# Starting a dense projection pass beside the first stage of a convolution: loads, slots and instruction order

## The chip, the cores and the metric

The kernel runs on one core of a Trainium2 chip. The metric is device time in microseconds, taken as the median of several runs. Before the change it is 2254.98 us (three runs, 2247.01 to 2256.77). The profiled execution of the same kernel spans 2245.5 us; all stage times below are from that execution.

## What is computed

Two unrelated halves, side by side in the output. Half A is a long convolution: `kv = shift(k) * v` (a filter of four taps along the sequence), then `y = irfft(rfft(kv) * rfft(ssm_k)) + kv * ssm_D`, then `q * y`, for 2048 rows and 1024 columns. Half B is a recurrence over 64 segments of 32 rows with a memory of 8 rows:

```
for s in range(n_seg):
    h = concatenate([mem, xs], axis=1)          # 8 memory rows, 32 rows of x
    q, k, v = h @ Wq, h @ Wk, h @ Wv            # 32 heads of 128
    p = softmax(mask(q @ k.T * scale))
    o = (p @ v) @ Wo
    mem = o[:, :M]; outs.append(o[:, M:])
```

All inputs and outputs are bfloat16.

## The kernel before, in words

Half A is `a_kernel`, a Fourier transform in three stages. Stage 1 (lines 229 to 259) walks 16 row tiles. For each, TensorE transposes a tile of ssm_k (line 233), VectorE forms the shifted product u (lines 252 to 258), TensorE applies the first transform to both (line 223), ScalarE copies the result out of PSUM (line 225), and the sync queue stores it to the DRAM scratch tensors SK and SU (line 226). Ahead of the loop stand tables of sines, built on VectorE, ScalarE and GpSimd (lines 102 to 216). Stage 2 (lines 306 to 345) gathers sets of Kg and Ug from that scratch; it can begin only when all of it has been stored. For each of 33 units it does two small transforms, four products on VectorE (lines 326 to 329, the first is called pa), and two matmuls back (z, lines 341 and 343), and stores to SZ. Stage 3 (lines 371 to 380) reads SZ, makes y, multiplies by q and stores half A's output.

Half B is `b_kernel`. Ahead of its recurrence stands a dense pass over the last 8 rows of each segment, which are 512 rows in all and do not depend on the memory. XBT holds them transposed (lines 502 to 510). The weights are cut into chunks of 128 x 2048 (512 KB): chunk (m, kc, g) is matrix m (0 for K, 1 for Q, 2 for V), rows kc, half g of the heads. A group (m, g) needs 8 chunks. For each of 16 heads it does a chain of 8 matmuls of 128 x 512 into PSUM (line 554, tile kb_ps), a copy to a stage tile, alternately on ScalarE and VectorE (lines 542 and 544), and at its end one store of 2 MB into the DRAM tensor REC (line 559). Each run of bytes in that store is 128 columns, 256 bytes, long.

After each of the four K and Q groups come four x blocks (lines 528 to 535): a load of 128 rows of x into X_sb (two buffers; even blocks on the sync queue, odd ones on GpSimd's), 8 transposes (xt_ps), a copy to xt (two buffers), and a store to REC. Then come the V groups (line 573, vb_ps), whose results go to the DRAM tensor VBD. The recurrence (from line 750) then reads REC, VBD and the weights.

Of the 64 weight chunks, 21 do not fit and are streamed in every segment through a ring of six slots from the DRAM tensor WS (line 629). The others stay resident: 12 in the pool Wmid, which is open from the end of stage 1, 19 in Wres, whose space is free only after stage 3, and 12 in Wlate, loaded after the V groups. In the dense pass, chunks that have no resident place yet are loaded into a ring of 8 slots called pw. A streamed chunk is copied from there into WS on GpSimd's queue (line 523).

The order of the program text is not the order on the engines. A scheduler with its own cost estimates places the instructions of each engine when the program is built, except in the recurrence, where the order is written out by hand. Every engine, and every DMA queue's issuing engine, then works in its own order, and waits on semaphores. In the built program before, group (0, 0), 128 matmuls, lies beside stages 2 and 3; the groups (0, 1), (1, 0), (1, 1), all x blocks but one, and the V groups come after stage 3's last matmul.

The functions that the change touches, with the line numbers of the profile:

Of the kernel before, what the change touches and what calls it, by code (L numbers as in the profile page):

```python
# [9 lines left out]
BF = mybir.dt.bfloat16  # L10
# [21 lines left out]
def a_kernel(ctx: ExitStack, tc, q, k, v, shift_k, ssm_k, ssm_D, outa, spare, stage1_done):  # L32
# [32 lines left out]
    with ExitStack() as c1:  # L65
        cw = c1.enter_context(tc.tile_pool(name="a_cw", bufs=1, side="right"))
        io = c1.enter_context(tc.tile_pool(name="a1_io", bufs=3, side="right"))
        k0pool = c1.enter_context(tc.tile_pool(name="a1_k0", bufs=6, side="right"))
        wk = c1.enter_context(tc.tile_pool(name="a1_wk", bufs=3, side="right"))
        ps_big = c1.enter_context(tc.tile_pool(name="a1_ps", bufs=3, space=PSUM))  # L70
# [6 lines left out]
        v_i = cw.tile([128, NP, 32], I32, name="v_i")  # L77
        nc.gpsimd.iota(v_i[:], pattern=[[2, NP], [128, 32]], base=0, channel_multiplier=0)
# [4 lines left out]
        shflat = cw.tile([1, 4096], BF, name="shflat")  # L83
# [3 lines left out]
        KS = []  # L87
        for db in range(8):
            KS.append(spare())
            (nc.sync if db % 2 == 0 else nc.scalar).dma_start(KS[db][:], ssm_k[db * 128:(db + 1) * 128, :])  # L90
# [97 lines left out]
        for M, n in ((Mre, nxr), (Mim, nxi)):  # L188
            nc.gpsimd.memset(M[:], 0.0)
            aM = cw.tile([128, NP, 32], I32, tag="aM", name="aM")  # L190
            nc.vector.tensor_scalar(out=aM[:], in0=v_i[:], scalar1=p_mod32[:, 0:1], scalar2=n[:, 0:1], op0=ALU.mult, op1=ALU.add)
            nc.vector.tensor_scalar(out=aM[:], in0=aM[:], scalar1=4095, scalar2=None, op0=ALU.bitwise_and)
            sM = cw.tile([128, NP, 32], BF, tag="sM", name="sM")
            act_sin(sM[:], aM[:], 12)
            nc.gpsimd.memset(sM[32:64, 0, :], 0.0)
            for (r0, c0) in [(0, 0), (64, 32)]:
                nc.gpsimd.tensor_copy(M[r0:r0 + 64, :, c0:c0 + 32], sM[r0:r0 + 64])
# [6 lines left out]
        aNi = cw.tile([128, NS, 32], I32, name="aNi")  # L204
        nc.vector.tensor_tensor(out=aNi[:], in0=w_f[:].unsqueeze(2).to_broadcast([128, NS, 32]),
                                in1=kcol_f[:, 0:32].unsqueeze(1).to_broadcast([128, NS, 32]), op=ALU.mult)
        for N, ph in ((Nre, (1024, 0)), (Nim, (2048, 1024))):
            nc.gpsimd.memset(N[:], 0.0)
            aN = cw.tile([128, NS, 64], I32, tag="aM", name="aN")
            for x in range(2):  # L210
                nc.vector.tensor_scalar(out=aN[:, :, 32 * x:32 * x + 32], in0=aNi[:], scalar1=ph[x], scalar2=None, op0=ALU.add)
            nc.vector.tensor_scalar(out=aN[:], in0=aN[:], scalar1=4095, scalar2=None, op0=ALU.bitwise_and)
            sN = cw.tile([128, NS, 64], BF, tag="sM", name="sN")
            act_sin(sN[:], aN[:], 12)
            for (r0, c0) in [(0, 0), (32, 64), (64, 0), (96, 64)]:
                nc.gpsimd.tensor_copy(N[r0:r0 + 32, :, c0:c0 + 64], sN[r0:r0 + 32])
# [12 lines left out]
        for t in range(16):  # L229
            pt = ps_t.tile([128, 1024], BF, tag="ktp", name="k_tp")  # L230
            for db in range(8):
                src = KS[db][:].rearrange("p (n r) -> p r n", r=16)[:, t, :]
                nc.tensor.transpose(pt[:, db * 128:(db + 1) * 128], src, ident[:])
            kt = wk.tile([128, 1024], BF, tag="kt", name="kt")
            nc.scalar.copy(kt[:], pt[:])
            if t == 0:
                nc.vector.tensor_tensor(out=kt[0:1, :], in0=kt[0:1, :], in1=Drow[0:1, :], op=ALU.add)
            stage1(kt, t, SK1)
            K0 = k0pool.tile([128, 1024], BF, tag="K0", name="K0")
            load_rows(K0, k, t, 0, nc.sync)  # L240
            ktiles[t] = K0
            Vt = io.tile([128, 1024], BF, tag="Vt", name="Vt")
            load_rows(Vt, v, t, 0, nc.gpsimd)
            acc = wk.tile([128, 1024], BF, tag="uacc", name="uacc")
            for li, lag in enumerate((3, 2, 1, 0)):
                if t - lag >= 0:
                    Kl = ktiles[t - lag]
                else:
                    Kl = io.tile([128, 1024], BF, tag="Kx", name="Kx")
                    load_rows(Kl, k, t, lag, nc.sync)  # L250
                if li == 0:
                    nc.vector.tensor_tensor(out=acc[:], in0=Kl[:], in1=SH[:, lag, :], op=ALU.mult)
                else:
                    pr = wk.tile([128, 1024], BF, tag="prod", name="prod")
                    nc.vector.tensor_tensor(out=pr[:], in0=Kl[:], in1=SH[:, lag, :], op=ALU.mult)
                    nc.vector.tensor_tensor(out=acc[:], in0=acc[:], in1=pr[:], op=ALU.add)
            u = wk.tile([128, 1024], BF, tag="u", name="u")
            nc.vector.tensor_tensor(out=u[:], in0=acc[:], in1=Vt[:], op=ALU.mult)
            stage1(u, t, SU1)
# [123 lines left out]
def b_kernel(ctx: ExitStack, tc, x, mem0, Wq, Wk, Wv, Wo, outb, n_seg, run_a):  # L383
# [26 lines left out]
    first_used = [ch for m, g in groups for ch in resident if ch[0] == m and ch[2] == g]  # L410
    parts = [first_used[:N2], first_used[N2:N2 + N3]]
# [40 lines left out]

    c0p = ExitStack()
    pools = {}

    def stage1_done():
# [4 lines left out]
        pools["ps0"] = c0p.enter_context(tc.tile_pool(name="b0_ps", bufs=2, space=PSUM))  # L461
# [31 lines left out]
    run_a(pw, stage1_done)  # L493

    wres3 = ctx.enter_context(tc.tile_pool(name="b_wres", bufs=1, reuse_waits="tile"))
    for i, ch in enumerate(parts[1]):
        res[ch] = wres3.tile([128, 2048], BF, name=f"Wres{i}")[:]

    ps0 = pools["ps0"]
    with c0, c0p:  # L500
        xq = [nc.sync, nc.gpsimd]
# [10 lines left out]
        def group(m, g):  # L512
            ws = []
            for kc in range(8):
                ch = (m, kc, g)
                if ch in res:
                    nc.sync.dma_start(res[ch], dram_chunk(ch))
                    ws.append(res[ch])
                else:
                    t = pw()  # L520
                    nc.sync.dma_start(t[:], dram_chunk(ch))
                    if ch in streamed:
                        nc.gpsimd.dma_start(stream_src(ch), t[:])
                    ws.append(t[:])
            return ws

        def x_block(b):
            X_sb = st.tile([128, 1024], BF, tag="X_sb", name="X_sb")
            xq[b % 2].dma_start(X_sb[:], x[b * 128:(b + 1) * 128, :])
            tp = ps0.tile([128, 1024], BF, tag="ps0", name="xt_ps")  # L530
            for kc in range(8):
                nc.tensor.transpose(tp[:, kc * 128:(kc + 1) * 128], X_sb[:, kc * 128:(kc + 1) * 128], ident[:])
            xt = st.tile([128, 4, 8, SEG], BF, tag="xt", name="xt")
            nc.vector.tensor_copy(xt[:], tp[:].rearrange("p (k j t) -> p j k t", k=8, j=4))
            nc.gpsimd.dma_start(REC[:, 4 * b:4 * b + 4, 0:256], xt[:].rearrange("p s k t -> p s (k t)"))

        flip = [0]

        def evac(dst, src):
            flip[0] ^= 1  # L540
            if flip[0]:
                nc.scalar.copy(dst, src)
            else:
                nc.vector.tensor_copy(dst, src)

        nxb = 0
        for m in (0, 1):
            for g in range(2):
                ws = group(m, g)
                stage = st.tile([128, n_seg, 16, 8], BF, tag="stage", name="stage")  # L550
                for hl in range(16):
                    ps = ps0.tile([128, 512], F32, tag="ps0", name="kb_ps")
                    for kc in range(8):
                        nc.tensor.matmul(ps[:], lhsT=ws[kc][:, hl * 128:(hl + 1) * 128],
                                         rhs=XBT[:, kc].rearrange("p s t -> p (s t)"),
                                         start=(kc == 0), stop=(kc == 7))
                    evac(stage[:, :, hl, :], ps[:].rearrange("p (s t) -> p s t", t=8))
                o = 256 * (m + 1) + 128 * g
                nc.sync.dma_start(REC[:, :, o:o + 128], stage[:].rearrange("p s h t -> p s (h t)"))
                for _ in range(n_blk // 4):  # L560
                    x_block(nxb)
                    nxb += 1
# [17 lines left out]


# [352 lines left out]
def kernel(  # L934
# [22 lines left out]
    def run_a(spare, stage1_done):  # L957
        with ExitStack() as ctx_a:
            a_kernel(ctx_a, tc, A_q[0], A_k[0], A_v[0], A_shift_k, A_ssm_k, A_ssm_D, outa, spare, stage1_done)
# [41 lines left out]
```

## Time and profile before

| stretch | us | what runs in it |
|---|---|---|
| stage 1 | 0 to 124.4 | 16 row tiles; last transform matmul at 122.7 |
| gap | 124.4 to 138.5 | first gathers; XBT |
| stage 2 | 138.5 to 253 | 33 units, 50 kb matmuls between them |
| stage 3 | 253 to 305 | 64 y matmuls, the other 78 kb matmuls of the group |
| three groups and their x blocks | 305 to 439.1 | 384 kb matmuls, the remaining x blocks |
| V groups | 439.1 to 498 | 256 vb matmuls |
| late weights, ring start | 498 to 519 | 12 chunks and the first 6 of the ring |
| recurrence | 519 to 2245 | 64 segments, 1218 streamed chunks |

TensorE's share of busy time over the span is 77%, VectorE's 40%, ScalarE's 28%. These are means over stretches that differ in what bounds them, so the stretches are read one by one. A line of the profile that begins with SPq, ACTq or POOLq is an instruction that only issues a DMA; its duration is the time that the issuing engine was held, not that of the transfer.

### The profile page before, as it was taken

Reading aid. Unit: us, or ns where it says so; the run is one execution under the profiler, and the core shown is the slowest. Engines: PE = TensorE matmul, PEld = TensorE weight load, DVE = VectorE, ACT = ScalarE, POOL = GpSimd, SP = SyncE. Lnnn points to the kernel's source line nnn. Section 1 sums busy time; section 2 is a strip of 40 time slices with the busy share of each in tenths; the row PEclk is TensorE's granted clock in tenths of the full one; section 3 lists DMA queues with packets and bytes.
Section 4 is the critical chain, followed back from the end, with each engine's and each line's share of the span. In section 5 each row is a group of like instructions: output and inputs, shape, how many; then the busy total and the mean of one; then the engine's idle time right before and its main releaser. Section 6 shows DMA issues by size and latency. Waiting matters only on the chain. (4 is left out here: it accounts for less than half of the span.)

```text
span 2245.5 us, 81488 instructions
## 1 busy us (share of the span) xinstructions
PE 1738.0 (77%) x35636; PEld 932.4 (42%) x35636; DVE 889.0 (40%) x2702; ACT 630.7 (28%) x1111; POOL 429.2 (19%) x1115
## 2 busy tenths in 40 slices
PE   4667767886787877888888888887877878888886
PEld 2222223333444444444444444444444444444443
DVE  9948632122333333333333333333333333333333
ACT  5856301112222222222222222222222222222222
POOL 7123311100111111211111112111111111122111
PEclk9789989897999999999999999999999999999999
DMA  7999698649999999999999999999999999999997
GB/s 247 358 364 323 216 323 276 171 112 395 392 393 370 388 391 380 388 389 387 396 391 395 395 392 390 393 393 381 394 385 369 383 391 392 386 389 390 392 390 266
DMA packets 293133, 803.59 MB, mean 358 GB/s; under 512 B 84812, under 2 KB 84844, under 8 KB 292775
## 3 DMA queue, kind: packets, MB, share of 16 engines
q1 hardware_dynamic: 262440, 734.16, 86.2%
q0 software_dynamic: 23536, 50.51, 6.6%
q10 hardware_dynamic: 6800, 13.72, 1.8%
q8 instruction: 278, 4.55, 0.8%
q14 instruction: 79, 0.65, 0.1%
HBM read 738.87 MB, written 62.39 MB: 357 GB/s over the span
## 5 line engine op out<-in xcount | busy, mean ns | idle before, releaser
L777 PEld LDWEIGHTS <-rec 128*32 128x32 bf16 x12351 | 319.5, 96 | 475.1 <-issue 255.1
L777 PE MATMUL acc<-wring,rec 128*32 128x512 bf16 (+1 forms) x3777 | 374.3, 386 | 136.9 <-DMA wring<-WS 121.8
L786 ACT CAST qkv_sb<-acc 128x512 bf16<-128x512 f32 x384 | 225.1, 586 | 672.0 <-PE acc L777 672.0
L777 PE MATMUL acc<-Wres,rec 128*32 128x512 bf16 x4864 | 382.3, 383 | 0.0
L863 PEld LDWEIGHTS <-OT 128*32 128x32 bf16 x8192 | 215.3, 96 | 174.8 <-issue 148.7
L777 PE MATMUL acc<-Wmid,rec 128*32 128x512 bf16 x3072 | 237.8, 384 | 0.9 <-issue 0.9
L863 PE MATMUL yacc<-Wlate,OT 128*32 128x256 bf16 x5120 | 219.6, 273 | 12.4 <-issue 11.4
L863 PE MATMUL yacc<-wring,OT 128*32 128x256 bf16 x3072 | 153.3, 275 | 97.0 <-DMA wring<-WS 57.4
L723 PEld LDWEIGHTS <-OTB 128*16 128x16 bf16 x4096 | 104.3, 89 | 104.7 <-issue 96.3
L879 DVE COPY KT<-tps 128x512 bf16<-128x512 bf16 x64 | 27.2, 425 | 291.2 <-PE tps L792 291.2
L849 ACT CAST OT<-OTp 128x512 bf16<-128x512 f32 x128 | 75.0, 586 | 236.9 <-PE OTp L841 236.7
L678 POOL DMA_DIRECT2D rec<-REC x64 | 37.3, 583 | 531.8 <-issue 270.3
L850 DVE CAST OTB<-OTp 128x128 bf16<-128x128 f32 x128 | 37.3, 291 | 255.3 <-ACT OT L849 255.3
L618 DVE TENSOR_SCALAR wring<-OTp 128x384 int32<-128x384 int32 x126 | 112.2, 891 | 59.7 <-PE acc L777 54.1
L753 POOL COPY KT<-rec 128x128 bf16<-128x128 bf16 x128 | 38.5, 301 | 454.5 <-PE SB L801 436.3
L723 PE MATMUL SB<-Wlate,OTB 128*16 128x256 bf16 x2480 | 95.7, 274 | 35.8 <-DVE SB L714 19.7
L807 DVE TENSOR_REDUCE mx<-SB 128x5 f32<-128x200 f32 x128 | 47.1, 368 | 190.4 <-PE SB L801 190.4
L738 POOL DMA_DIRECT2D out_dram<-YB x128 | 73.2, 578 | 233.6 <-DVE YB L736 220.1
L723 PE MATMUL SB<-wring,OTB 128*16 128x256 bf16 x1488 | 77.7, 273 | 39.4 <-DVE SB L702 32.9
L792 PE MATMUL tps<-ident,qkv_sb 128*128 128x128 bf16 x1024 | 101.2, 221 | 7.9 <-ACT qkv_sb L786 0.2
L792 PEld LDWEIGHTS <-qkv_sb 128*128 128x128 bf16 x1024 | 62.8, 97 | 105.5 <-ACT qkv_sb L786 63.4
L926 POOL DMA_DIRECT2D out_dram<-Y x64 | 45.5, 711 | 238.2 <-ACT Y L919 227.1
(216 smaller groups left out, 2412.6 us busy)
## 6 DMA issues: line engine op xcount, KB each, us to landing
wring<-WS SPq DMA_DIRECT2D x1218, 512.0 KB, 7.3
rec<-REC POOLq DMA_DIRECT2D x64, 192.0 KB, 6.1
SK<-s_sb SPq DMA_DIRECT2D x16, 512.0 KB, 5.3
SU<-s_sb SPq DMA_DIRECT2D x16, 512.0 KB, 4.8
Kg<-SK ACTq DMA_DIRECT2D x32, 256.0 KB, 5.5
Ug<-SU SPq DMA_DIRECT2D x32, 256.0 KB, 5.6
REC<-stage SPq DMA_DIRECT2D x4, 2048.0 KB, 18.1
SZ<-zs SPq DMA_DIRECT2D x31, 256.0 KB, 5.2
```

The lines of the kernel that those rows point to most:

```text
L618: nc.vector.tensor_scalar(out=dst, in0=src, scalar1=0, scalar2=None, op0=ALU.bitwise_or)
L678: nc.gpsimd.dma_start(rec[:], REC[:, s, :])
L723: nc.tensor.matmul(self.acc[32 * dq:32 * dq + W, x - o:y - o], lhsT=self.OTB[:, c, 4 * g + i, :], rhs=r, start=first and not self.seeded, ...
L738: nc.gpsimd.dma_start(bass.AP(outb.tensor, outb.offset + (SEG * NB * self.b + NX) * 2048 + 256 * dq, [[2048 * SEG, NB], [2048, 8], [1, 256 ...
L753: nc.gpsimd.tensor_copy(KT[:, :, :, 32:40], KBs[:, 128 * g:128 * g + 128].rearrange("p (c i t) -> p i c t", c=4, i=4))
L777: nc.tensor.matmul(self.acc[32 * c:32 * c + 32, x - 512 * c:y - 512 * c], lhsT=hT[:, kc, :], rhs=r, start=(kc == 0 and x == 512 * c), stop ...
L786: nc.scalar.copy(sb[:], self.acc[:])
L792: nc.tensor.transpose(tp[:, i * 128:(i + 1) * 128], sb[:, i * 128:(i + 1) * 128], ident[:])
L807: nc.vector.tensor_reduce(out=mx[:], in_=S, op=ALU.max, axis=AX.X)
L849: nc.scalar.copy(OT[:], o_view[:, :, :, 0:32])
L863: nc.tensor.matmul(yacc[32 * dq:32 * dq + 32, x - o:y - o], lhsT=OT[:, c, i, :], rhs=r, start=(h == 0 and x == o), stop=(h == 31), tile_po ...
L926: nc.gpsimd.dma_start(bass.AP(outb.tensor, outb.offset + SEG * s * 2048, [[256, 4], [2048, 32], [1, 256]]), Y[:])
```

## The change

The dense pass is to begin earlier. XBT and group (0, 0) are put where stage 1 ends, so that the scheduler can place them beside stage 1; the groups (0, 1), (1, 0) and (1, 1) follow beside and after stages 2 and 3. For this, weight slots and PSUM are needed while stage 1 runs. The V tiles of half A's first eight row tiles now use slots of the ring pw, and as each is used up, its slot takes a chunk of group (0, 0). The rows of ssm_k, which had lain in that ring, get a buffer of their own, paid for by fewer buffers in the other pools of stage 1. The sine tables' integers and the shift filter lie in the two stage tiles, which are free until the first group needs one.

Since Wmid now serves groups (0, 1) and (1, 0), and Wres the V chunks, eight K and Q chunks of Wres (`extra`) are loaded after their group has gone through, for the recurrence. The x blocks come in sets of five, five and six after three groups.

The core of the diff:

```diff
-        io = c1.enter_context(tc.tile_pool(name="a1_io", bufs=3, side="right"))
-        k0pool = c1.enter_context(tc.tile_pool(name="a1_k0", bufs=6, side="right"))
+        io = c1.enter_context(tc.tile_pool(name="a1_io", bufs=2, side="right"))
+        k0pool = c1.enter_context(tc.tile_pool(name="a1_k0", bufs=5, side="right"))
-        ps_big = c1.enter_context(tc.tile_pool(name="a1_ps", bufs=3, space=PSUM))
+        ps_big = c1.enter_context(tc.tile_pool(name="a1_ps", bufs=2, space=PSUM))
...
-        v_i = cw.tile([128, NP, 32], I32, name="v_i")
+        ints = slot16([128, 4096], I32, "ints")
+        v_i = ints[:, 0:32 * NP].rearrange("p (a b) -> p a b", b=32)
...
-        shflat = cw.tile([1, 4096], BF, name="shflat")
+        shflat = slot16([1, 4096], BF, "shflat")
-        KS = []
+        KS = cw.tile([128, 8, 2048], BF, name="KS_nat")
...
-            kt = wk.tile([128, 1024], BF, tag="kt", name="kt")
+            kt = wk.tile([128, 1024], BF, tag="kt", bufs=2, name="kt")
-            Vt = io.tile([128, 1024], BF, tag="Vt", name="Vt")
+            Vt = slot4()[:, 0:1024] if t < 8 else io.tile([128, 1024], BF, tag="Vt", name="Vt")[:]
...
-    first_used = [ch for m, g in groups for ch in resident if ch[0] == m and ch[2] == g]
-    parts = [first_used[:N2], first_used[N2:N2 + N3]]
+    own = {mg: [ch for ch in resident if ch[0] < 3 and (ch[0], ch[2]) == mg] for mg in groups}
+    parts = [(own[0, 1] + own[1, 0])[:N2], own[2, 0] + own[2, 1]]
+    extra = [ch for ch in own[0, 0] + own[1, 1] + resident if ch not in parts[0] + parts[1]][:N3 - len(parts[1])]
+    parts[1] = parts[1] + list(dict.fromkeys(extra))
...
     def stage1_done():
...
-        pools["ps0"] = c0p.enter_context(tc.tile_pool(name="b0_ps", bufs=2, space=PSUM))
+        make_xbt()
+        dense(0, 0)
...
-        nxb = 0
-        for m in (0, 1):
-            for g in range(2):
-                ws = group(m, g)
...
-                for _ in range(n_blk // 4):
-                    x_block(nxb)
-                    nxb += 1
+        for n, (m, g) in enumerate(((0, 1), (1, 0), (1, 1))):
+            dense(m, g)
+            for b in range(5 * n, min(5 * n + 5, n_blk)):
+                x_block(b)
+        x_block(n_blk - 1)
...
+        for ch in parts[1]:
+            if ch in extra:
+                nc.sync.dma_start(dst_view(res[ch], ch), dram_chunk(ch))
```

The tiles uacc, prod and u of stage 1 also go from three buffers to two. The recurrence is unchanged, but for which of its resident chunks lie in which pool.

## The prediction

> **What bounds the kernel now.** I read the table of stages first: one query for busy time, granted clock and DMA share in stretches cut at the stage borders (columns: stretch, its length, busy us and instructions of PE, PEld, DVE, ACT, POOL, then clock, DMA share, GB/s).
>
> ```profile
> 50.00:124.40 74.40, 44.34 (x166) 16.86 (x164) 60.60 (x112) 58.29 (x63) 10.18 (x19) 0.75 0.99 363
> 124.40:138.50 14.10, 6.03 (x40) 3.63 (x42) 0.00 (x0) 3.97 (x6) 1.08 (x2) 0.53 1.02 359
> 138.50:253.00 114.50, 88.80 (x445) 26.81 (x442) 96.31 (x173) 72.39 (x137) 45.72 (x43) 0.94 0.82 290
> ...
> 319.50:348.30 28.80, 28.80 (x130) 12.76 (x128) 5.53 (x8) 4.69 (x8) 3.68 (x6) 0.96 0.99 371
> 348.30:360.10 11.80, 3.10 (x35) 2.66 (x33) 2.67 (x4) 0.00 (x0) 2.58 (x4) 0.69 1.09 377
> 360.10:389.10 29.00, 29.00 (x129) 12.81 (x128) 5.53 (x8) 4.69 (x8) 3.13 (x5) 0.95 0.61 186
> 389.10:398.30 9.20, 3.12 (x33) 2.39 (x32) 1.98 (x3) 0.00 (x0) 2.05 (x3) 0.75 1.00 273
> 398.30:429.10 30.80, 29.98 (x129) 13.10 (x129) 6.22 (x9) 4.69 (x8) 2.61 (x4) 0.91 0.40 108
> 429.10:439.10 10.00, 3.08 (x34) 2.37 (x33) 2.67 (x4) 0.00 (x0) 2.04 (x3) 0.78 0.99 269
> ...
> 519.00:2245.00 1726.00, 1381.63 (x33981) 784.95 (x33981) 622.10 (x2240) 441.23 (x833) 301.25 (x953) 0.99 1.00 385
> ```
>
> The last row is the segment loop: DMA share 1.00, for 1726 us. It streams the same 1218 chunks before and after, so only its start can move. Ahead of it: stage 1 to 124.4 (from 50 us on its DMA share is 0.99), a gap of 14.1 in which stage 2 waits for its first gathers, stage 2 (114.5, DVE busy 96.3), stage 3 to 305, and then the tail, where PE alone works through dense groups of 29 to 31 us with sets of transposes of x (9 to 12 us, PE a third busy) between them, and the V pass until 498. In gap, groups, sets and V pass, one engine's delay is everybody's.
>
> Next, the instructions in order of time on the sync queue, to see what a set waits for (start, duration of the issue):
>
> ```profile
> 389.75 0.33 SPq L529 DMA_DIRECT2D X_sb<-in_B_x_dram  x1
> 390.18 0.52 SPq L559 DMA_DIRECT2D REC<-stage  x1
> 394.32 9.81 SPq L529 DMA_DIRECT2D X_sb<-in_B_x_dram  x1
> ...
> 300.23 0.57 SPq L559 DMA_DIRECT2D REC<-stage  x1
> 304.82 7.91 SPq L380 DMA_DIRECT2D out_dram<-ot  x2
> 313.15 0.87 SPq L529 DMA_DIRECT2D X_sb<-in_B_x_dram  x1
> ```
>
> An x load issued behind the 2 MB store of a group is stuck: at 394.32 its issue alone takes 9.81, until 14.0 after the store (404.13 - 390.18). Behind the store at 300.23 the x load goes out at 313.15 and PE, waiting for it, resumes at 317.73, 17.5 after the store. In the three later sets that late load is not needed: with two X_sb buffers a set of four needs two loads inside itself, and the one on SP is issued just ahead of the store.
>
> [...] a chain of 8 takes 1.73 us, a group of 128 takes 28.8. [...] The group's store writes runs of 256 B (128 columns of bf16), and the page's DMA part gives it 18.1 us for 2 MB (116 GB/s, against 385 in the loop).
>
> **The change, part by part.** I compared the order of instructions of the two built programs.
>
> 1. Stage 1. The ssm_k rows get their own buffer, V tiles 0 to 7 use the weight ring, the integer tables use the stage slots; several pools lose a buffer (K0 6 to 5, Kx 3 to 2, s1_ps 3 to 2). The 32 transposes for XBT and their 4 ACT copies (1.0 us each) move in, and 2 more weight chunks are loaded in it. The first table phase: shift filters now come after two kt copies, and the third Kx load waits for a Kx slot and for POOL's table copies (5.5 and 5.8 us), so u of row tile 1, at 40.4 before, moves to about 43. From there each tile takes 4.82 of DVE and 4.8 of ACT (1.03 + 4 x 0.94), and DMA is full. 2 chunks are 1 MB or 3 us at 363 GB/s; some V loads move out ahead of 50 us and give 1 to 2 back. 15 kb matmuls stand between the last s1 matmuls, and the eighth needs a chunk issued only after SU 13: up to 4 us of PE wait. I take +4; bounds 0 (all hidden in the waits that ACT has already) and +10.
>
> 2. The gap. After the last s1 matmul PE has 113 kb matmuls in a row ahead of the first Kre: 113 x 0.2157 = 24.4, plus about 1 for evacuations behind Kg issues on ACT. PE is in order, so stage 2's first products come some 27.5 after stage 1's last matmul (24.4 + 1 + the 2 that Kre, Ure and the copies take). Before: 138.56 - 122.7 = 15.9. So +11.5; bounds +9 and +14. This is what is paid for the group; the gap's 14 us are what is hidden.
>
> 3. Start of stage 2. The same 50 kb matmuls are spread over it as before. But group (0,1)'s two ring chunks need slots of (0,0), so are issued only at the end of the gap; PE meets them right behind unit 1, before the first z: about 3.5 of wait. Then SP issues the 2 MB store of (0,0) ahead of the first SZ stores and the fourth set's Ug: stuck for about 14, landing about 17 to 20 after, when three preloaded sets (6 units of 2.73 to 3.3) are used up: 0 to 5. Against that, the early stalls of DVE in this stage (idle 114.5 - 96.3 = 18 in all) shrink, as three sets are loaded. I take +2; bounds -7 and +8.
>
> 4. Stage 3: same order, same 78 kb beside it and just ahead. 0.
>
> 5. The tail. One group leaves it: the built order has 256 kb after the last y matmul, not 384: -29.5 (28.8, 29.0, 30.8: mean). The 16 x blocks are now in sets of 5, 5 and 6 behind three groups, not four sets of 4. So every set needs a third round of loads:
>  - set 1 (the rest of it 14.5 before): its fifth block is one more load, as at 318.79, issued behind two weight chunks: +3, and xt has two buffers, so that block's copy waits for the REC store of block 2: +1.5. Total 19.
>  - set 2: blocks 5 and 6 are ready, 7 comes by POOL, but 8 is on SP behind the store. Store at 1.1 after the group, landing of X_sb 17.5 later, two blocks more: about 21, not 11.8.
>  - set 3: two chunks (1 MB, 2.7 us) go ahead of the store, so block 12 lands at 1.1 + 2.7 + 17 = 20.5; block 14 can be issued only then and lands 4 later; 15 comes by POOL after the REC store of 12; the xt copies of 14 and 15 wait for stores of 12 and 13 (6 us to land): about 28, not 10.
>  Sets after: 19 + 21 + 28 = 68; before: 14.5 + 11.8 + 9.2 + 10.0 = 45.5: +22.5. Tail: -29.5 + 22.5 = -7. Bounds: -19 (17 and 20 for sets 2 and 3, 1.5 less in set 1) and +1.
>
> 6. The 8 extra chunks loaded a second time (4 MB, 11 us of DMA) lie in group and V pass, where DMA is 0.4 to 0.6 busy: 0, but for the chunk counted ahead of set 3's store. 12 late chunks and the ring's first 6 follow the V pass as before: 0. Other residents in the loop: same bytes streamed, 0.
>
> Sum: 4 + 11.5 + 2 + 0 - 7 = +10.5, which I round up to +12, since each wait leaves PE at the cold clock for its first chain (+1.7), and three such waits are new or longer. 2255 + 12 = 2267.
>
> **The rivals.** A: the group's removal is worth its full length and more, because the x loads land early: three sets of some 13 take 39 in place of 45.5, so the tail gains 36; with +11.5 in the gap and +4 in stage 1 it is -20.5: 2234. For it: the x loads are small and DMA is half idle there; set 3 and set 4 of before wait only 3 to 4 us at a time. Against: those loads stood ahead of the store in the ring. B: no change. The ring wait costs half (sets 2 and 3 together 38), because a store with nothing beside it drains in less than the 14 to 15.6 seen: tail -18, sum near +1: 2256. For it: the store of 430.16 was beside little traffic, and the rec load waited for it only until 445. Against: that is 15 us too. C: much slower: stage 1 is held by its smaller pools (+10) and stage 2 by the store at its start (+8), sum 10 + 14 + 8 - 7 = +25: 2280. For it: DMA at 0.99 in stage 1 and both new loads in it.
>
> **How the numbers follow.** My forecast 0.35, C 0.12, B 0.30, A 0.23. Slower by over 0.5% (above 2266.3) takes C and most of my own case, with its lower edge in "same": 0.44. Same (2243.7 to 2266.3): B and that edge, 0.33. Faster: A, 0.23. The likeliest is slower at 2267. The range goes down to 2238, leaving out the better half of A, and up to 2288, beyond C by its spread.
>
> **What would show it.** In the changed profile: 113 kb matmuls without a break in the gap and the first pa some 27 after the last s1 matmul (12 fewer if I am wrong on the gap); an X_sb issue of 9 us or more behind the stores of groups (1,0) and (1,1), with PE idle before xt_ps on DMA for some 12 in set 2 and 15 to 20 in set 3; V pass starting about 127 after the last y matmul, not 134. If sets 2 and 3 together take under 30, A is right. If pa comes later than 144 + 12 because stage 1's last matmul is past 132, it is C.

## The result, and the profile after

The changed kernel takes 2279.7 us (median of 4 runs, 2272.0 to 2288.4), the kernel before 2251.1 (median of 4, 2247.0 to 2256.8): ratio 1.0126, 95% interval 1.008 to 1.0173. It is slower, as forecast, but by 28.6 us between the medians, where 12 were forecast. The profiled executions have spans of 2245.5 and 2269.6, 24.1 apart; those 24 us can be placed.

First the table of stages of the changed kernel, cut at its own stage borders (columns as in the prediction).

```profile
50.00:138.00 88.00, 47.88 (x235) 22.23 (x234) 62.56 (x114) 63.41 (x70) 23.83 (x19) 0.92 0.89 320
138.00:165.00 27.00, 25.65 (x125) 11.49 (x124) 5.54 (x8) 6.32 (x11) 0.00 (x0) 1.00 0.98 357
165.00:284.50 119.50, 89.61 (x439) 27.00 (x436) 96.72 (x173) 71.43 (x136) 47.38 (x46) 0.92 0.84 285
...
388.00:409.00 21.00, 3.65 (x42) 3.10 (x41) 3.36 (x5) 0.00 (x0) 3.91 (x6) 0.65 0.94 250
409.00:437.80 28.80, 28.80 (x130) 12.80 (x129) 5.53 (x8) 4.68 (x8) 2.59 (x4) 0.96 0.19 57
437.80:464.30 26.50, 4.96 (x50) 4.14 (x49) 4.05 (x6) 0.00 (x0) 5.04 (x8) 0.58 0.97 276
543.80:2269.60 1725.80, 1385.62 (x33981) 790.91 (x33981) 622.73 (x2240) 440.69 (x833) 301.06 (x953) 0.99 1.00 385
```

The gap is now full of PE work, 25.65 of 27.0, and 27 long. The two later sets of x blocks (388 to 409 and 437.8 to 464.3) last 21 and 26.5 with PE busy for 4 to 5. Stage 1 ends at 138, and its DMA share fell to 0.89. The loop is what it was.

Read stage by stage, from the times of six instructions in each trace (end of the last stage 1 matmul, first product of stage 2, end of the last z matmul, end of the last y matmul, first V matmul, first recurrence matmul):

| us | stage 1 | gap | stage 2 | to last y | tail to V pass | V pass to loop | loop |
|---|---|---|---|---|---|---|---|
| before | 122.7 | 15.8 | 113.6 | 52.9 | 134.0 | 79.8 | 1726.6 |
| after | 138.0 | 27.1 | 119.4 | 53.3 | 126.5 | 79.5 | 1725.8 |
| difference | +15.3 | +11.3 | +5.8 | +0.4 | -7.5 | -0.3 | -0.8 |
| forecast | +4 | +11.5 | +2 | 0 | -7 | 0 | 0 |

Gap and tail came as forecast; stage 1 did not. The sync queue of the changed kernel, in order of time, as in the prediction:

```profile
164.71 0.52 SPq L562 DMA_DIRECT2D REC<-stage  x1
175.33 4.60 SPq L290 DMA_DIRECT2D SZ<-zs  x1
...
388.91 0.56 SPq L562 DMA_DIRECT2D REC<-stage  x1
389.56 13.23 SPq L533 DMA_DIRECT2D X_sb<-in_B_x_dram  x1
...
438.71 0.52 SPq L562 DMA_DIRECT2D REC<-stage  x1
439.33 13.56 SPq L533 DMA_DIRECT2D X_sb<-in_B_x_dram  x1
```

An x load behind a group's store holds SP for 13.2 and 13.6 us, and the first SZ store is done with its issue at 179.93, 15.2 after the store of group (0,0). PE's side of it, and of stage 1 (PE instructions in order of time; the bracket is the idle time before, and what ended it):

```profile
63.23 0.48 PE L512 MATMUL xbt_ps<-ident,X_sb 128*128 128x128 bf16 x3 [11.25 <-POOL ident masks.py:199]
...
80.69 0.50 PE L512 MATMUL xbt_ps<-ident,X_sb 128*128 128x128 bf16 x3 [7.33 <-DMA X_sb<-in_B_x_dram]
...
146.46 17.46 PE L557 MATMUL kb_ps<-XBT,pw 128*128 128x512 bf16 x80 [1.35 <-ACT stage L546]
163.85 0.41 PE L310 MATMUL Kre_ps<-Kg,Mre 128*64 128x512 bf16 x2
...
407.14 1.89 PE L536 MATMUL xt_ps<-ident,X_sb 128*128 128x128 bf16 x16 [13.84 <-DMA X_sb<-in_B_x_dram]
...
455.37 1.89 PE L536 MATMUL xt_ps<-ident,X_sb 128*128 128x128 bf16 x16 [16.06 <-DMA X_sb<-in_B_x_dram]
```

The first two lines are new and no step of the prediction has them: inside stage 1, PE stands for 11.3 us until POOL has built the identity, and for 7.3 until an x tile has landed, because the transposes for XBT are now in the middle of its queue. Behind it, DVE stalls in turn, first for PE and then for a K tile (its instructions in order of time):

```profile
62.34 0.68 DVE L259 TENSOR_TENSOR prod<-K,SH 128x1024 bf16<-128x1024 bf16 x1
67.89 0.69 DVE L262 TENSOR_TENSOR u<-uacc,pw 128x1024 bf16<-128x1024 bf16 x1 [4.86 <-PE s_ps L227]
...
78.52 0.69 DVE L259 TENSOR_TENSOR prod<-K,SH 128x1024 bf16<-128x1024 bf16 x1 [8.74 <-DMA K<-in_A_k_dram]
```

and POOL's instruction that PE waits for, first in the changed kernel, then in the kernel before:

```profile
47.49 15.69 POOL masks.py:199 TENSOR_SCALAR_AFFINE_SELECT ident<-ident 128x128 bf16<-128x128 bf16 x1
```

```profile
44.94 0.49 POOL masks.py:199 TENSOR_SCALAR_AFFINE_SELECT ident<-ident 128x128 bf16<-128x128 bf16 x1
```

It is the same instruction on the same 128 x 128 tile. It ends at 63.18, 0.16 after the DVE product of 62.34 ended. DVE stopped there because its next instruction waited for PE, and PE stood waiting for POOL.

### The profile page after: what moved, and what is told of

Same layout as the page of the kernel before. It is cut to its first block, busy times and chain, and to the rows that moved or that the text cites. A ratio compares the mean times of both kernels' runs of the same rounds, so it can differ in the third digit from the quotient of the medians.

```text
span 2269.6 us, 81502 instructions
## 1 busy us (share of the span) xinstructions
PE 1737.5 (77%) x35636; PEld 938.0 (41%) x35636; DVE 889.3 (39%) x2702; ACT 628.2 (28%) x1110; POOL 444.0 (20%) x1115
## 5 line engine op out<-in xcount | busy, mean ns | idle before, releaser
L794 PEld LDWEIGHTS <-rec 128*32 128x32 bf16 x12351 | 324.2, 96 | 467.0 <-issue 251.8
L794 PE MATMUL acc<-Wres,rec 128*32 128x512 bf16 x4864 | 395.7, 383 | 1.2 <-issue 1.1
L794 PE MATMUL acc<-Wmid,rec 128*32 128x512 bf16 x3072 | 224.9, 382 | 0.0
L740 PE MATMUL SB<-Wlate,OTB 128*16 128x256 bf16 x2480 | 97.2, 281 | 33.7 <-DVE SB L731 20.3
L943 POOL DMA_DIRECT2D out_dram<-Y x64 | 45.5, 711 | 239.6 <-ACT Y L936 236.6
```

What stands on the lines that cost most here:

```text
L740: nc.tensor.matmul(self.acc[32 * dq:32 * dq + W, x - o:y - o], lhsT=self.OTB[:, c, 4 * g + i, :], rhs=r, start=first and not self.seeded, ...
L794: nc.tensor.matmul(self.acc[32 * c:32 * c + 32, x - 512 * c:y - 512 * c], lhsT=hT[:, kc, :], rhs=r, start=(kc == 0 and x == 512 * c), stop ...
L943: nc.gpsimd.dma_start(bass.AP(outb.tensor, outb.offset + SEG * s * 2048, [[256, 4], [2048, 32], [1, 256]]), Y[:])
```

## The experiments

Each edit lets the scheduler place other instructions anew, so an edit in one stage can shift group matmuls in another; where that bears on a reading it is said. Single executions of one kernel differ by over 1% (55 of the kernel before lie between 2241 and 2273; in the profiled runs the loop alone takes 1721 to 1737), so totals are medians, and stages are read from the traces, one execution of each kernel. Counts of group matmuls in a stage are those recorded there; a few records are missing from each trace. A group matmul is counted as 0.2157 us: in the kernel before, those from 404.27 to 418.94 us start that far apart (14.67 us for 68, granted clock 1.00). Behind a set's wait for x they start further apart: 0.426 us in the kernel before from 399.50 to 402.91 (3.41 us for 8, granted clock 0.50 from 399.1 to 403.3), which is 1.7 more than a chain's 1.73 and is the prediction's cold clock. All of it in one table, the same columns as above; "ratio" is to the kernel before.

| run | stage 1 | gap | stage 2 | to last y | tail | median us | ratio (95%) |
|---|---|---|---|---|---|---|---|
| before | 122.7 | 15.8 | 113.6 | 52.9 | 134.0 | 2251 to 2256 | 1 |
| after | 138.0 | 27.1 | 119.4 | 53.3 | 126.5 | 2279.7 | 1.0126 (1.008-1.0173) |
| e1 | 134.4 | 26.0 | 119.8 | 55.4 | 124.3 | 2268.8 | 1.0072 (1.0053-1.0092) |
| e2 | 137.2 | 25.6 | 119.5 | 52.0 | 104.1 | 2253.6 | 0.9997 (0.9975-1.0018) |
| e3 | 139.2 | 13.5 | 105.5 | 53.9 | 145.0 | 2266.0 | 1.0057 (1.0038-1.0075) |
| e4 | 125.2 | 16.3 | 111.9 | 52.9 | 137.9 | 2257.5 | 1.001 (0.9986-1.0033) |
| e5 | 132.9 | 24.2 | 118.2 | 53.3 | 134.1 | 2274.1 | 1.01 (1.0081-1.012) |
| e6 | 138.2 | 25.6 | 123.8 | 55.7 | 92.6 | 2247.2 | 0.9971 (0.9956-0.9986) |
| e7 | 135.3 | 22.3 | 123.8 | 52.1 | 131.1 | 2265.8 | 1.0056 (1.0032-1.008) |
| b1 | 131.6 | 24.3 | 120.8 | 59.9 | 74.7 | 2225.0 | 0.9886 (0.9854-0.9918) |
| b2 | 122.4 | 16.5 | 110.5 | 53.6 | 108.7 | 2223.3 | 0.9871 (0.985-0.9891) |
| b3 | 136.8 | 22.3 | 121.3 | 55.4 | 73.7 | 2227.3 | 0.9874 (0.9827-0.9921) |
| b4 | 137.7 | 12.3 | 108.7 | 81.3 | 86.8 | 2235.0 | 0.9913 (0.9883-0.9943) |
| b5 | 126.2 | 24.2 | 123.2 | 57.0 | 82.8 | 2225.3 | 0.987 (0.9845-0.9895) |

**e1: the identity.** The changed kernel, with

```diff
-        make_identity(nc, ident[:])
+        nc.vector.tensor_copy(ident[:], a_ident[:])   # stage 1's own identity
```

> The changed kernel with one edit: the 128x128 identity that the XBT transposes read is copied on DVE from stage 1's own identity, not built on POOL. Theory 1 (in the changed kernel PE stands 11.3 us in stage 1 because POOL's 128x128 select for that identity is held off by DVE's back-to-back products, 15.69 us against 0.49 before, and the K loads issued late because of it cost DVE 8.7 more): the wait is gone, the last stage 1 matmul comes at 125 to 129 in place of 138.0, total 2270 (2264 to 2274). Rival (the smaller pools and the two added loads hold stage 1, and the identity's wait only covers that): last stage 1 matmul at 134 or later, total 2277 to 2282.

The wait for POOL is gone, yet stage 1 ends at 134.4, only 3.6 earlier and on the rival's side of the line. PE's queue in e1:

```profile
65.31 0.50 PE L512 MATMUL xbt_ps<-ident,X_sb 128*128 128x128 bf16 x3 [11.18 <-DMA X_sb<-in_B_x_dram]
```

The wait for an x tile, 7.3 before, has taken the identity's place. So the total fell into the expected range without the expected reason: the identity is one of two things that the same transposes lack, and taking one away lays the other bare.

**e2: the x loads.** The changed kernel, with

```diff
-        xq[b % 2].dma_start(X_sb[:], x[b * 128:(b + 1) * 128, :])
+        nc.gpsimd.dma_start(X_sb[:], x[b * 128:(b + 1) * 128, :])
```

> The changed kernel with one edit: all 16 x blocks are loaded by the POOL queue, so none stands in SP's ring behind a group's 2 MB store. Theory 1 (ring order is what makes sets 2 and 3 long): PE's wait of 13.8 us in set 2 and of 16.1 in set 3 falls to 3 to 6 each, set 2 from 21.0 to 11 to 15, set 3 from 26.5 to 14 to 18, total 2279.7 - 16 = 2264 (2258 to 2269). Rival (the 16 engines are busy with the store whatever queue the load comes from): waits of 11 or more stay, total 2276 to 2282. Stage 1 and the gap are as in the changed kernel.

PE's instructions are in the same order as in the changed kernel, so this is a clean comparison. Set 2 takes 14.0 (from 21.0), set 3 20.5 (from 26.5; 14 to 18 were expected), and the tail is 22 shorter. PE's waits for x loads in the tail fall from 50.8 us in all to 30.9, the longest from 16.1 to 6.4. Those in set 2 of e2:

```profile
378.52 1.03 PE L536 MATMUL xt_ps<-ident,X_sb 128*128 128x128 bf16 x8 [3.18 <-DMA X_sb<-in_B_x_dram]
381.68 1.03 PE L536 MATMUL xt_ps<-ident,X_sb 128*128 128x128 bf16 x8 [2.12 <-DMA X_sb<-in_B_x_dram]
386.81 1.03 PE L536 MATMUL xt_ps<-ident,X_sb 128*128 128x128 bf16 x8 [4.10 <-DMA X_sb<-in_B_x_dram]
```

A store of 2 MB in SP's ring (the DMAs that SP issues) holds up a load in POOL's much less than one behind it in its own: PE's three waits in this set are of 2.1 to 4.1 us, where one was 13.8 in the changed kernel. How the two rings are served side by side no run shows. The total fell by 26, to below the expected range, since set 1 gained too: its x load, issued at 344.09 in the changed kernel behind the store of group (0,1) and two out stores, made PE wait 10.4 there and 6.4 here.

**e3: the group put back.** XBT, buffers and weights as changed, but group (0,0) beside stages 2 and 3 and sets of four:

```diff
         make_xbt()
-        dense(0, 0)
...
     run_a(pw, slot16, stage1_done)
+    dense(0, 0)
```

> The changed kernel with the first group (K, half 0) put back beside stages 2 and 3, and x blocks in four sets of four; XBT, the buffers and the weight split stay as changed. Theory 1 (113 matmuls in the gap cost 11.2 us of it): first product of stage 2 comes 14 to 17 after the last stage 1 matmul in place of 27.1, stage 1 still ends near 138, last y matmul to V pass 134 in place of 126.7, total 2279.7 - 11.5 - 4 + 8 = 2272 (2267 to 2278). Rival (the gap is set by the gathers' round trip in the fuller DMA queues, the group lay in it for nothing): the gap stays at 24 or more and the total rises by the tail's 8, to 2286 or more.

The scheduler still put 46 of the group's 128 matmuls ahead of stage 2's first product, 30 of them in the gap. With 30 in place of some 113 the gap shrinks to 13.5, so it was the matmuls that made it 27.1, and the rival falls. Stage 2 shrinks as well, by 13.9, of which 34 fewer group matmuls in it (17, not 51) explain at most 34 x 0.2157 = 7.3. The tail grows by 18.5, to 145.0 where 134 was expected: the x loads, half of them still in SP's ring, make PE wait 43.6 there, 32.0 in the kernel before. Taken together what the early group adds costs 13.6 + 13.9 and saves 18.5. The total, 2266.0, is just below the expected range.

**e4: the small pools alone.** The kernel before, with

```diff
-name="a1_io", bufs=3 ... name="a1_k0", bufs=6 ... name="a1_ps", bufs=3
+name="a1_io", bufs=2 ... name="a1_k0", bufs=5 ... name="a1_ps", bufs=2
-tag="kt" / "uacc" / "prod" / "u"           (three buffers)
+tag="kt" / "uacc" / "prod" / "u", bufs=2
```

> The kernel before with nothing of the change but stage 1's smaller pools (Kx 3 to 2 with Vt, K0 6 to 5, kt, sums, products and u 3 to 2, PSUM 3 to 2). Theory 1 (pools cost little, a few us at the start): last stage 1 matmul at 123 to 127 (122.7 before), total within 4 us of the kernel before, 2251 to 2255. Rival (the pools are what made stage 1 15 us longer): last stage 1 matmul at 131 or later, total 2259 or more.

Stage 1 ends 2.5 later. The pools alone are a small part of the 15.3. The total is 2.5 above the expected range, and not told apart from the kernel before (0.9986 to 1.0033).

**e5: all x tiles of XBT loaded early.** e1, with

```diff
+        shflat = slot16([1, 4096], BF, "shflat")     # now ahead of the integers
...
+        XS = slot16([128, 4, 1024], BF, "XS")        # in the slot of the shift filters
         for tb in range(4):
-            X_sb = st.tile([128, 1024], BF, tag="X_sb", name="X_sb")
+            X_sb = XS[:, tb, :]
```

> Run e1 (identity copied on DVE) with one more edit: the four x tiles of XBT are loaded into one 8 KB tile in the slot that the shift filters leave at about 14 us, so no load waits for a transpose and all are sent while DMA is idle. Theory 2 (after e1: PE runs in order, and the XBT transposes inside stage 1 make it wait for whatever they lack, first the identity, without it X_sb, 11.2 us in e1): no wait for X_sb, last stage 1 matmul at 126 to 130 (134.4 in e1, 138.0 in the changed kernel), total 6 less than e1's 2269, 2263 (2258 to 2267). Rival (the K loads in a full DMA hold stage 1: DVE waits 12.3 us for them in e1): last stage 1 matmul at 133 or later, total 2266 to 2271.

Stage 1 ends at 132.9, the rival's side of the line: PE's wait for x fell to 6.5 in two pieces, and 10.2 of the 15.3 us were still there. The total, 2274.1, is above both ranges and 5 worse than e1's: the tail is 9.8 longer, with two more x blocks and 13 more group matmuls in it. Theory 2 falls as the whole explanation. What e5 and the kernel before have in common shows in one row of each, the stretch from 40 us to the end of stage 1 (first before, then after, then e5):

```profile
40.00:122.70 82.70, 50.57 (x196) 19.87 (x196) 70.60 (x125) 63.49 (x69) 17.49 (x30) 0.78 0.95 344
```

```profile
40.00:138.00 98.00, 53.47 (x252) 24.22 (x252) 72.56 (x129) 67.69 (x74) 33.73 (x33) 0.93 0.89 316
```

```profile
40.00:132.90 92.90, 57.02 (x251) 25.09 (x251) 73.88 (x131) 68.92 (x75) 18.11 (x32) 0.83 0.96 344
```

Multiply length by GB/s: 28.4 MB before, 31.0 after, 32.0 in e5. Before and e5 move them at the same 344 GB/s with DMA 0.95 busy, so e5 is longer as its bytes are: 3.5 MB / 344 GB/s = 10.2. The changed kernel has 2.5 MB more, 7.3 us at that rate, and moves them at 316, which is the other 8.0. That alone doesn't show what is cause: a stretch of full DMA that lasts longer for another reason also takes in more bytes that were waiting to be sent. For that b5, below, takes bytes away. The DMA issues of stage 1, before and then after (count, KB each), say which bytes:

```profile
pw<-in_B_Wk_dram SPq DMA_DIRECT2D x5, 512.0 KB, 6.8
...
X_sb<-in_B_x_dram SPq DMA_DIRECT2D x1, 256.0 KB
X_sb<-in_B_x_dram POOLq DMA_DIRECT2D x1, 256.0 KB, 3.5
```

```profile
pw<-in_B_Wk_dram SPq DMA_DIRECT2D x8, 512.0 KB, 7.5
...
X_sb<-in_B_x_dram SPq DMA_DIRECT2D x3, 256.0 KB
X_sb<-in_B_x_dram POOLq DMA_DIRECT2D x3, 256.0 KB, 6.5
```

Three weight chunks and four x tiles more: 3 x 0.52 + 4 x 0.26 = 2.6 MB.

**e6: the first store on POOL.** e2, with

```diff
-        nc.sync.dma_start(REC[:, :, o:o + 128], stage[:]...
+        (nc.gpsimd if (m, g) == (0, 0) else nc.sync).dma_start(REC[:, :, o:o + 128], stage[:]...
```

> Run e2 (x loads on POOL) with one more edit: the 2 MB store of group (0,0), issued at the start of stage 2, goes by the POOL queue in place of SP. Theory 1 (that store, in SP's ring ahead of the SZ stores and the next Ug loads, is what makes stage 2 six us longer than before): stage 2 from first product to last z matmul takes 112 to 115 in place of 119.5, total 2254 - 5 = 2249 (2245 to 2251). Rival (the group's chunks and evacuations, or DMA as a whole, make it longer): 118 to 121, total within 2 of e2's 2254.

The total came as theory 1 has it, but not from stage 2, which took 123.8: the scheduler put 32 more group matmuls in it (6.9 us), and 11.5 came off the tail because a whole set of x blocks moved ahead of the last y matmul (which itself came 3.8 us later after the last z). Even less those 6.9, stage 2 is 116.9, not 112 to 115. So SP's ring is not shown to be what makes stage 2 longer; the run doesn't settle it.

**e7: six K0 tiles.** e5, with `a1_k0` at 6 buffers again.

> Run e5 with one more edit: six K0 tiles in stage 1 as in the kernel before, in place of five. Theory 3 (what is left of stage 1's delay in e5 is that with five tiles a K load goes out hardly more than one row tile ahead, and with the added loads ahead of it lands late: DVE waits for K 12.9 us in all): DVE's waits for K fall under 4 us in all, last stage 1 matmul at 124 to 128 in place of 132.9, total 2274 - 7 = 2267 (2262 to 2270). Rival (DMA is full in stage 1 whatever the tiles, 2 MB more have to pass): last stage 1 matmul at 131 or later, total 2271 or more.

DVE's waits (engine, line, waited for: total, times, longest), first in e5, then in e7:

```profile
DVE prod L259 <- DMA K<-in_A_k_dram: 12.9, 5, 5.6
```

```profile
DVE u L262 <- DMA Vt<-in_A_v_dram: 4.0, 1, 4.0
DVE prod L259 <- DMA K<-in_A_k_dram: 2.1, 1, 2.1
```

The wait for K is nearly gone and stage 1 is no shorter, 135.3. Theory 3 falls: the K waits were where the delay showed, not what made it. The total, 2265.8, lies in theory 3's range, but without its reason. The profiled execution was the slowest of ten; stage 1 is as long in b3 and b4, which have six K0 tiles too (136.8 and 137.7). That is also a limit of the sum of bytes: these three move 31.8 to 32.0 MB, as much as e5 and b1, at 328 to 334 GB/s, and take 2 to 6 us longer. Why the rate is lower there is open.

**b1: everything mended.** e5 with e2's and e6's edits, and the last twelve x blocks put between the chains of groups (1,0) and (1,1):

```diff
+            for b in blocks.get(hl, ()):
+                x_block(b)
...
+        dense(1, 0, {2 * i + 3: (4 + i,) for i in range(6)})
+        dense(1, 1, {2 * i + 3: (10 + i,) for i in range(6)})
```

> The change with everything mended at once: identity on DVE and early XBT loads (e5), x loads and the first store on POOL (e6), and the last twelve x blocks put between the chains of groups (1,0) and (1,1), one after every second chain, not in sets behind them. Theory: stage 1 128 (-9 against e2), stage 2 114 (-5), last y to V pass 22 x 0.2157 + 2 x 28.8 + 12 x 2.2 = 89 in place of 104 (-15): 2254 - 29 = 2225 (2217 to 2236), below both kernels. Rival (the x loads and stores only move to another place in a DMA that has no room): 2244 or more.

2225.0, as expected, and below both kernels, but that the sum came out to the microsecond is luck, since the parts differ: stage 1 131.6 and stage 2 120.8 gained less than expected, the tail (74.7, not 89) more. Against e6, whose x loads are on POOL too, the tail is 18 shorter: that is what the spreading adds.

**b2: the kernel before, its tail mended.** The same spreading of x blocks and POOL loads in the kernel before, one block behind chains 6, 10, 14 and 16 of each of the last three groups.

> The kernel before with only the tail mended: x loads on POOL, and the x blocks of the last three sets put between chains of their groups. Theory (the sets of before wait only 3 to 4 us at a time, so little is to be had without the change): tail 134 to 128 or 129, total 2252 - 5 = 2247 (2243 to 2251). Rival (spreading the blocks is worth as much here as in b1, the early group nothing): 2238 or less.

2223.3: I was wrong by 24 us, and the rival is right. The tail went from 134.0 to 108.7. PE's waits for x in the tail, first before, then b2:

```profile
PE xt_ps L532 <- DMA X_sb<-in_B_x_dram: 32.0, 6, 12.1
```

```profile
PE xt_ps L532 <- DMA X_sb<-in_B_x_dram: 4.3, 1, 4.3
```

From 314.6 to 411.7 PE does three groups and twelve blocks: 97.1 - 384 x 0.2157 = 14.3, or 1.2 us a block, where I had 2.2. In the sets of before, 15 blocks (one stood ahead of the last y matmul) cost 45.5, 3.0 each. Between chains a load has longer to land (the first two of these blocks start at 327.84 and 335.69, 7.9 apart); PE's longest wait in these 97 us is 0.3, and its granted clock 0.97, against 0.90 in the same stretch of before (319.5 to 429). The run changes two things, the queue of the loads and their places, and how much each is worth in this kernel no run shows.

**b3: b1 with six K0 tiles.**

> Run b1 (everything mended) with six K0 tiles in stage 1. Theory 3: stage 1 about 5 shorter, 2225 - 5 = 2220 (2215 to 2224). Rival (DMA is full): 2224 or more.

2227.3, the rival's side, though four runs between 2215 and 2238 do not tell 2220 from 2227. What decides is stage 1, which became 5 longer, 136.8, and not 5 shorter.

**b4: ten of the sixteen chains in the gap.** b3, with the first group's last six chains behind stage 3's code:

> Run b3 with one more edit: only the first 10 of the 16 chains of group (0,0) are begun in stage 1, the other 6 come after stage 3's code in the order, so they fill stages 2 and 3 and the store of the group goes out later. Theory (the gap holds about 15 us of matmuls for nothing, what is more is paid for): 50 matmuls in the gap in place of 98, gap 14 to 17 (b1: 24.2), stage 2 no longer beside the group's store, 110 to 115 (b1: 120.8), the moved 48 matmuls cost up to 10 later; total 2220 - 10 = 2210 (2203 to 2217). Rival (work is only moved, the same PE time is paid later): within 3 of b3.

Gap (12.3) and stage 2 (108.7, against 118.2 in e5 with the same 35 group matmuls in it) are a little shorter than expected, but the total is no better than b3's (8 worse, within the noise of the two): the 48 matmuls and the group's store now lie in stage 3, where PE waited 29.3 us for zt loads (21.5 in b1), and which grew by 26; the tail grew by 13, as all 16 x blocks are in it, not 12. The work was only moved.

**b5: the Wo copies moved out of stage 1.** b1, with

```diff
-        dense(0, 1)
+        late_tile = dense(0, 1)          # dense now returns its stage tile
...
         for ch in ring_order:
             if ch[0] == 3:
+                nc.gpsimd.dma_start(stream_src(ch)[0:1, 0:8], late_tile[0:1, n_seg - 1, 15, :])
                 nc.gpsimd.dma_start(dst_view(stream_src(ch), ch), dram_chunk(ch))
```

> Run b1 with one more edit: the six 512 KB copies of Wo chunks into the ring's DRAM buffer, which run in stage 1 in every kernel so far, are made to wait for the last chain of group (0,1) by an 8-element store into the same place, so 3.1 MB leave stage 1 for the time of groups (1,0) and (1,1). Theory 4 (from 40 us on stage 1 takes as long as its DMA bytes: 28.4 MB in 82.7 us before, 32.0 in 92.9 in e5, 32.1 in 91.6 in b1, all at 0.95 to 0.97 share): 29 MB left, last stage 1 matmul at 122 to 126 in place of 131.6, total 2225 - 7 = 2218 (2211 to 2223). Rival (waits between the engines set it, DMA is full only because they wait): last stage 1 matmul at 130 or later, total 2223 to 2231.

The stretch from 40 us to the end of stage 1, first b1, then b5:

```profile
40.00:131.60 91.60, 55.25 (x251) 23.91 (x251) 73.94 (x132) 68.28 (x75) 18.08 (x32) 0.87 0.97 350
```

```profile
40.00:126.20 86.20, 55.68 (x251) 23.73 (x251) 73.45 (x131) 68.12 (x75) 14.15 (x26) 0.84 0.94 333
```

Stage 1 ends at 126.2, 5.4 earlier than in b1 and just outside the expected 122 to 126, with 86.2 us x 333 GB/s = 28.7 MB in place of 91.6 x 350 = 32.1. So bytes in this stage do cost time, and the rival's 130 falls; but the 3.4 MB are 9.7 us at b1's rate, of which 5.4 were won, and the rate fell. The sum of bytes is a large part of the account, not all of it. POOL's queue, which also loads V, lost these copies too, but that is not what helped: DVE waited 0.2 us for V in b1 and 1.8 in b5, and for K 12.7 and 6.1. The total doesn't move (2225.3, in the rival's range), since the copies now stand in POOL's queue among the x loads (tail +8.1: PE waits 15.2 us for x there, 8.2 in b1).

## Why the prediction was right, and where it was not

The direction was right, but the sum was nearly 13 too low (2267 against 2279.7), and by the sign that the prediction named for it (last stage 1 matmul past 132, first product past 156), it was rival C that came: 138.0 and 165.1, and its 2280 is the time measured. The range held the time because its upper edge was drawn for C, to which a chance of 0.12 was given; for the forecast's own sum that is luck. C's number is in part luck too: the smaller pools that were to hold stage 1 cost 2.5 of its 15.3 us (e4), while the full DMA and the new loads, which C named beside them, did matter.

1. **Stage 1** is the step that failed: +4 with bounds 0 and +10, measured +15.3. "2 chunks are 1 MB or 3 us": 2.5 MB more pass before its end, 7.3 us at 344 GB/s, because four x tiles and a third chunk come in as well; b5 shows that bytes taken out of the stage shorten it, by about half of what they are at that rate. The rest, 8.0, is a lower rate, while engines waited for each other: PE for the identity and for an x tile. With these waits taken away in turn the rate rose from 316 to 330 (e1) and 344 (e5), and the stage became 3.6 and then 1.5 shorter, less than 8.0, as 1 MB more came into it. So the split into bytes and waits is worked out from rates; no edit took out one without touching the other. Of the 15.3 us, 8.9 were still there in b1, and 3.5 in b5. The prediction looked for delays in pools and loads, and took the order of instructions without asking what each added PE instruction waits for. That u of tile 1 comes near 43 was right (43.7), and the pools alone are 2.5 (e4).
2. **The gap**: +11.5 forecast, +11.3 measured, 113 matmuls with one break of 1.35; e3 and b4 show that they are the cause.
3. **Stage 2**: +2 forecast, +5.8 measured, within its bounds. PE waited 2.1, not 3.5, for the two chunks; SP was stuck to 15.2 after the store, as forecast; the early stalls of DVE did not shrink. With equal group matmuls inside, stage 2 is longer when the group is finished just ahead of it: by 5.8 in the changed kernel (51 in both), and by 7.7 and 9.5 in e5 against b2 and b4 (35 in each). Whether its store, its chunks or both do that is open: e6 moved the store to another ring, but other work with it. With the store in POOL's ring, b3 is 12.6 longer than b4, of which 48 more matmuls inside are up to 10.4.
4. **Stage 3**: 0 forecast, +0.4.
5. **The tail**: -7 forecast, -7.5 measured, V pass 126.5 after the last y matmul against "about 127". Set 2 took 21.0 (21 forecast), set 3 26.5 (28), PE's longest waits 13.8 and 16.1 (12, and 15 to 20). e2 shows the cause: with the x loads in another ring the tail is 22 shorter and the whole change is worth nothing, ratio 0.9997.
6. **Reloads and loop**: 0 forecast, -1.1.

Rival A (x loads early, all of the group gained) and B fall with the tail's waits: sets 2 and 3 together took 47.5, where A asked for under 30 and B for 38. What they asked for can be had, as b1 shows; but b2 gives the same without the change (2225.0 and 2223.3). The early group takes 29 us of matmuls out of the tail, and pays for it in the gap, in stage 2 and in stage 1. The large gain in this tail was in the queue and the places of its x blocks.

Where the prediction says that "the page's DMA part" gives the store 18.1 us, it means the page of the profile: 18.1 is the median of four stores of the kernel before, from issue to landing, with whatever else was moving, and the 116 GB/s are worked out from it.

## What to carry to other kernels

Where work is moved into an earlier stage, add up what bytes it brings there and what each moved instruction waits for: the changed kernel put transposes and loads into a stage whose DMA was 0.95 busy from 40 us on, and PE stood 18.6 us for an identity and an x tile that nobody had needed so early. In this kernel short loads that PE waits for did better in another ring than a long store's (22 us of the tail, e2), and better spread between long chains than gathered in sets (18 us more, b1 against e6). When a wait is removed and the stage is nearly as long as before, look at the stage's DMA bytes and rate before the next wait.

## What the runs showed of the hardware that was not expected

POOL's select on a 128 x 128 bf16 tile took 0.49 us in the kernel before, and 15.69 in the changed kernel, where it ended 0.16 after the last of a chain of DVE's bf16 products. POOL's busy time from 40 us to the end of stage 1 goes the same way: 17.5 us in the kernel before, 17.9 in e4 and 16.9 in b2, against 33.7 in the changed kernel, 34.1 in e2 and 33.6 in e3. In the changed kernel the select lasted through some 26 DVE instructions (15.5 us at 0.60 each); in the kernel before it got in at 44.94, between products that were as close, and the DVE product of 45.20 took 0.77 in place of 0.68. That DVE's products held it off is a reading of these times; no run took the products away, so the cause is not shown. The chain ended only when DVE ran out of work, since PE waited for this very select: DVE's next instruction, at 67.89, waited 4.86 us for PE.
